# A fused attention, expert and gate kernel on one core: rounding, low halves and operand making re-divided between VectorE and GpSimd, and respread over the stages

## Chip, cores and metric

One Trainium2 chip, one core. The metric is the device time of one launch in microseconds. Engines are named as in the profile: PE is TensorE (PEld its weight loads), DVE VectorE, ACT ScalarE, POOL GpSimd, SP SyncE; SP issues most transfers.

## What is computed

All in fp32, B=4, H=8, S=576, D=64, so N=2304 tokens of 512:

```python
k_p, v_p = mean of 8 neighbours of k, v
x = softmax(q @ k_p.T / sqrt(D)) @ v_p                    # attention, heads side by side: (2304, 512)
p = domain_probs / domain_probs.sum(-1)
x = sum over 4 experts of p[:, e] * (relu(x @ w1[e]) @ w2[e])      # w1 512x1024, w2 1024x512
out = (((x @ g_w1) * (x @ g_w2)) @ w3) @ w_out            # g_w1, g_w2 512x1024, w3 1024x1024, w_out 1024x512
```

Four of the inputs (`moe2_*`) arrive as 8-byte floats.

## The kernel before

**Exact products.** A matrix is held as a high and a low half in the fast fp32 form; `hi_lo` (L111) makes the high half on ACT and the low half as source minus high on DVE, or on the engine that the caller names. `mm3` (L106) makes each product of three matmuls. One function serves all tiles, so the low halves all have line 113.

**Rounding.** The 8-byte inputs are made into 4-byte ones on the chip, in 80 steps of 256 columns. `Rounding.step` (L208) loads two words per number (`din`), runs seven DVE instructions (L219 to L225) on `dtmp`, two buffers, and one add on POOL (L226). The result is stored by the *next* step's `flush` (L202): `wo` and the gate columns directly (L752), w3 transposed on DVE first (L256). Where steps stand is written by hand: a table of hooks in the attention stage, `at_s1` and `at_s2` in the experts. The first 48 steps (`SCRATCH`) are `w_out` and w3, then come 32 for the gate weights.

**Attention and expert 0** run interleaved over six batches of 384 tokens, eight units of first and second products each, with a hook before and after each unit's second product. Hooks hold the pieces of attention: scores, exponentials, sums, the quotient on POOL (L433), transpositions, and `attend`, whose product PE writes and `hi_lo` splits into the batch's `x`. `START` sets the hook of each of the 18 tiles of 128 tokens. `accumulate0` (L723) evicts four banks at the end of a batch. At the end of the stage `weights_of` and `prepare_x` make the operands of expert 1.

**Experts 1 to 3** run over four batches of 576 tokens. First products use seven products instead of eight (`seven`, L664): `weights_of(j)` (L589) takes two tiles `raw` of w1, makes four sums on DVE into one tile `s` (L600 to L603; the tag "t" has one buffer, which `prepare_x` shares) and splits everything into a set of seven operands; `prepare_x` (L624) does the like for a batch of `x` (L630 to L633) and stores it for later experts, which read it back with `fetch_x` (L650). `seven` evicts on DVE (L670); ACT makes relu twice, POOL the low half `h` (L700). Second products run in two halves of eight steps, each on four of the eight PSUM banks, evicted by `accumulate` (L730 on DVE, an adding transfer from POOL at L731). The **last batch** of an expert also makes the next expert's four weight sets, in the first products from the second group on, and splits its eight rows of w2 in the second half. In the last batch of expert 3 the sets are the gate's, the rows are `wo`, and `prepare_x` makes the gate's first two operands.

**w3 stage and gate.** `w3_rows` (L937) splits sixteen rows of w3; 192 matmuls make w3 @ w_out. The gate stage makes two halves of the hidden columns, four batches each, first products with `seven` and then 128-token tiles of output, copied by ACT in the first half (L1046) and added by DVE in the second (L1043). Half 0's last batch (`swap`) makes the second half's weight sets.

Each engine runs its instructions in the order in which the program records them, and SP its transfers; a wait holds up all that stands behind it. A low half that the change moves is a call with or without `nc.gpsimd`:

```python
hi_lo(*(t[:, at:at + m].rearrange("p a b c -> p (a b c)") for t in wop_t[j]), src, nc.gpsimd)
```

## Time and profile before

| | before |
|---|---|
| median of 3 runs (lowest to highest) | 1362.57 us (1360.78 to 1363.24) |
| the profiled execution: its time, its span | 1363.6 us, 1361.9 us |
| PE busy | 1221.3 us, 90% |
| DVE, ACT, POOL busy | 843.9 us (62%), 372.4 (27%), 542.4 (40%) |
| mean granted TensorE clock | 0.949 |

The page gives busy times per engine and the groups of instructions; a busy PE is not PE at its peak. The table of windows gives, for a stretch of the span, each engine's busy time and the granted clock, 1.00 for 2.4 GHz and 0.5 for 1.2. The timeline names, behind each instruction, how long its engine stood idle before it and what ended that. Where a wait has several causes, the one that came last is named.

### The profile page before, as it was taken

What the parts mean: (1) busy time and instruction counts of PE and PEld (TensorE: products, weight loads), DVE (VectorE), ACT (ScalarE), POOL (GpSimd) and SP (SyncE); (2) the same over time, 40 slices, a digit from 0 to 9 for tenths busy, and PEclk for the clock granted to TensorE, in tenths of its full rate; (3) what the DMA queues carried; (4) which work ended last, traced back from release to release, by engine and by line L of the source; (5) the groups of instructions that cost most, each with busy time, mean ns of one, the idle gap of its engine ahead of it and who ended that gap; (6) DMA issues with size and microseconds to landing.
All of it is one profiled execution on the core that took longest, in us unless ns stands there. A gap on an engine that the chain in (4) does not pass through costs nothing.

```text
span 1361.9 us, 21447 instructions
## 1 busy us (share of the span) xinstructions
PE 1221.3 (90%) x7953; PEld 1156.3 (85%) x7953; DVE 843.9 (62%) x1765; ACT 372.4 (27%) x659; POOL 542.4 (40%) x534
## 2 busy tenths in 40 slices
PE   6889798989889987799998689999839999979997
PEld 4777787889889987799998689999828999879996
DVE  5758877745678774577675675767430776555453
ACT  3333122222423414323214131132322332321110
POOL 5544443142635536234336343344634332442121
PEclk8899898999899998899999889999869999989999
DMA  8776544443664763756663746655255144755441
GB/s 194 202 177 171 165 122 126 115 116 109 216 186 99 234 183 100 218 175 162 138 213 73 227 133 172 194 175 133 82 127 201 36 188 178 260 192 183 156 168 62
DMA packets 176508, 216.51 MB, mean 159 GB/s; under 512 B 50892, under 2 KB 126996, under 8 KB 176404
## 3 DMA queue, kind: packets, MB, share of 16 engines
q1 hardware_dynamic: 160564, 196.27, 44.8%
q0 software_dynamic: 15840, 18.88, 9.4%
...
HBM read 133.80 MB, written 81.30 MB: 158 GB/s over the span
## 4 chain that ended last, share of the span: by engine, by line
PE 60%; DVE 14%; DMA 10%; issue 7%; POOL 5%; SPq 3%; ACT 2%; DVEq 0%; POOLq 0%; ACTq 0%
PE g L107 9%; PE g L108 9%; PE g L109 9%; PE s L107 9%; PE s L109 9%; PE s L108 9%; POOL wl L113 2%; DMA stage<-in_q_dram 1%; DMA raw<-in_moe_w_dram 1%; DMA gate<-dtmp 1%; DMA din<-in_moe_w_dram 1%; PE w L108 1%; PE w L109 1%; PE x_ps L454 1%; PE w L107 1%
## 5 line engine op out<-in xcount | busy, mean ns | idle before, releaser
L107 PE MATMUL s<-xol,wh 128*128 128x288 f32 x980 | 297.6, 304 | 40.0 <-DVE part L730 34.6
L107 PE MATMUL g<-h,w2h 128*128 128x288 f32 (+1 forms) x960 | 298.5, 311 | 30.4 <-DVE u L670 17.5
L109 PE MATMUL s<-xoh,wh 128*128 128x288 f32 x980 | 295.1, 301 | 0.0
L108 PE MATMUL g<-h,w2l 128*128 128x288 f32 (+1 forms) x960 | 294.7, 307 | 0.0
L109 PE MATMUL g<-h,w2h 128*128 128x288 f32 (+1 forms) x960 | 294.5, 307 | 0.0
L108 PE MATMUL s<-xoh,wl 128*128 128x288 f32 x980 | 294.3, 300 | 0.0
L107 PEld LDWEIGHTS s<-xol,wh 128*128 128x128 f32 x980 | 188.6, 192 | 44.0 <-DVE part L730 36.3
L107 PEld LDWEIGHTS g<-h,w2h 128*128 128x128 f32 x960 | 184.2, 192 | 36.4 <-DVE u L670 18.5
L700 POOL TENSOR_TENSOR h<-c,h 128x576 fp32r<-128x576 f32 x96 | 140.1, 1480 | 143.7 <-ACT c L699 121.8
L108 PEld LDWEIGHTS s<-xoh,wl 128*128 128x128 f32 x980 | 189.2, 193 | 0.2
L109 PEld LDWEIGHTS s<-xoh,wh 128*128 128x128 f32 x980 | 188.8, 193 | 0.0
L108 PEld LDWEIGHTS g<-h,w2l 128*128 128x128 f32 x960 | 184.3, 192 | 0.0
L109 PEld LDWEIGHTS g<-h,w2h 128*128 128x128 f32 x960 | 184.0, 192 | 0.0
L226 POOL TENSOR_TENSOR dtmp<-dtmp 128x256 f32<-128x256 f32 x80 | 60.6, 757 | 240.1 <-DVE dtmp L225 199.0
L113 POOL TENSOR_TENSOR g<-c,g 128x576 fp32r<-128x576 f32 x32 | 47.3, 1479 | 196.4 <-ACT g L112 196.4
L698 ACT ACTIVATE h<-c 128x576 fp32r<-128x576 f32 x96 | 65.0, 677 | 197.7 <-DVE c L670 197.7
L672 ACT ACTIVATE x<-s 128x288 f32<-128x288 f32 x80 | 31.7, 397 | 197.6 <-PE s L109 197.5
L670 DVE TENSOR_TENSOR c<-s,v 128x288 f32<-128x288 f32 x160 | 69.1, 455 | 24.4 <-PE s L109 16.5
L670 DVE TENSOR_TENSOR u<-s,x 128x288 f32<-128x288 f32 x80 | 36.2, 453 | 75.7 <-ACT x L672 65.7
L107 PE MATMUL g<-xl,w 128*128 128x384 f32 x192 | 70.5, 367 | 0.5 <-DVE xl L113 0.5
L699 ACT ACTIVATE c<-c 128x576 f32<-128x576 f32 x96 | 65.8, 686 | 5.9
L108 PE MATMUL g<-xh,w 128*128 128x384 f32 x192 | 67.4, 351 | 0.0
...
## 6 DMA issues: line engine op xcount, KB each, us to landing
...
```

Of the source, the lines that this page charges most:

```text
L107: nc.tensor.matmul(ps, lh, rl, start=first, stop=False)
L108: nc.tensor.matmul(ps, ll, rh, start=False, stop=False)
L109: nc.tensor.matmul(ps, lh, rh, start=False, stop=last)
L113: (lo_eng or nc.vector).tensor_tensor(lo, src, hi.bitcast(F32), op=ALU.subtract)
L226: nc.gpsimd.tensor_tensor(a, a, b, op=ALU.add)
L454: nc.tensor.matmul(px[a * D:(a + 1) * D, off:off + n], vp_t[b][:NK, 2 * hp + a], at_t[i, hp // 2][:NK, 2 * (hp % 2) + a, off:off + n], sta ...
L670: nc.vector.tensor_tensor(to, one, two, op=ALU.add)
L672: nc.scalar.activation(x, product(j, A11, B11), AF.Copy)
L698: nc.scalar.activation(h[:, 0], r, AF.Relu)
L699: nc.scalar.activation(r, r, AF.Relu)
L700: nc.gpsimd.tensor_tensor(h[:, 1], r, h[:, 0].bitcast(F32), op=ALU.subtract)
```

## The change

- The add that ends a rounding step (L226) goes from POOL to DVE. The low halves in `prepare_x` (of `xr`), of A11, A12 and A22 in `weights_of`, of w3's rows, and of w2's rows in expert 1's first batch go from POOL to DVE. The low half of the four sums `s` and `h` stay on POOL.
- Rounding steps: in the attention stage 20 instead of 24, five in each of four batches; in expert 1's first three batches three each instead of five; in those of experts 2 and 3 seven instead of six; none in a last batch (expert 2's had five); three in the w3 stage and two in each of the first three batches of the gate stage, which had none.
- In a last batch set 0 is made in the first products, in two pieces, and sets 1 to 3 in the second products, a piece at every second step. The swap batch of the gate stage makes one piece per group and the rest afterwards; at the end of the attention stage the sets move by two units.
- Of the gate's first operands, one is made at step 3 of expert 3's last second products and one after them; two rows of w3 are split before the last eviction, a third of the rows in tiles with the tag "c".
- Attention: each batch makes the three tiles and the product of the next one, at the same places in all batches; pooling of k and v moves with it.

```diff
--- before.py
+++ after.py
@@ -225,3 +225,3 @@
             nc.vector.scalar_tensor_tensor(b, l, 2.0 ** -52, b, op0=ALU.mult, op1=ALU.mult)
-            nc.gpsimd.tensor_tensor(a, a, b, op=ALU.add)
+            nc.vector.tensor_tensor(a, a, b, op=ALU.add)
             self.done = a, sink
@@ -549,18 +549,19 @@
         hooks[6] = [(None, probs_T)]
-        START = {t: 3 * (t - TPB) if t < 2 * TPB else 6 + (55 * (t - 2 * TPB + 1)) // 12 for t in range(TPB, NTILE)}
-        for t, at in START.items():
-            hooks[at] += do_scores(t) + do_exps(t)
-            if t > TPB:
-                hooks[at + 1] += do_qT(t + 1)
-            one, two = do_normalise(t)
-            hooks[at + 1].append(one)
-            hooks[at + 2].append(two)
-            one, two = do_turn(t)
-            hooks[at + 4].append(one)
-            hooks[at + 5].append(two)
-            if t % TPB == TPB - 1:
-                for n, piece in enumerate(do_attend(t // TPB)):
-                    hooks[at + 5 + n].append(piece)
+        for i in range(1, NB):
+            base = PER * (i - 1)
+            for o in range(TPB):
+                t, at = TPB * i + o, base + 3 * o
+                hooks[at] += do_scores(t) + do_exps(t)
+                if t > TPB:
+                    hooks[at + 1] += do_qT(t + 1)
+                one, two = do_normalise(t)
+                hooks[at + 1].append(one)
+                hooks[at + 2].append(two)
+                one, two = do_turn(t)
+                hooks[at + 4].append(one)
+                hooks[at + 5].append(two)
+            for n, piece in enumerate(do_attend(i)):
+                hooks[base + 11 + n].append(piece)
         hooks[1] = do_qT(TPB + 1) + hooks[1]
-        for b, at_v, at_k in ((1, 3, None), (2, 25, 16), (3, 43, 33)):
+        for b, at_v, at_k in ((1, 3, None), (2, 30, 20), (3, 50, 39)):
             for n, piece in enumerate(do_v(b, GP)):
@@ -577,3 +578,3 @@
         for i in range(1, NB - 1):
-            for at in (0, 2, 5, 7, 10, 12, 14) if i < NB - 2 else (0, 3, 5):
+            for at in (0, 3, 6, 9, 14):
                 also.setdefault(PER * i + at, []).append(lambda: rounding.step(SCRATCH))
@@ -590,5 +591,5 @@
 
-            def split(src, at, m):
+            def split(src, at, m, eng):
                 src = src.rearrange("p a b c -> p (a b c)") if len(src.shape) == 4 else src.rearrange("p a c -> p (a c)")
-                hi_lo(*(t[:, at:at + m].rearrange("p a b c -> p (a b c)") for t in wop_t[j]), src, nc.gpsimd)
+                hi_lo(*(t[:, at:at + m].rearrange("p a b c -> p (a b c)") for t in wop_t[j]), src, eng)
 
@@ -603,7 +604,7 @@
                 nc.vector.tensor_tensor(s[:, 3], left[:, 2:], s[:, 1], op=sub)
-                split(left, A11, 2)
-                split(right[:, 2:], A22, 1)
+                split(left, A11, 2, nc.vector)
+                split(right[:, 2:], A22, 1, nc.vector)
                 stream.fill()
             if n != 0:
-                split(parts.pop(j), S1, 4)
+                split(parts.pop(j), S1, 4, nc.gpsimd)
 
@@ -633,4 +634,4 @@
             nc.vector.tensor_tensor(t[:, 3], r[:, 1, 0], t[:, 1], op=sub)
-            hi_lo(bh[:, 0], bl[:, 0], r[:, 0, 0], nc.gpsimd)
-            hi_lo(bh[:, 1:], bl[:, 1:], r[:, 1], nc.gpsimd)
+            hi_lo(bh[:, 0], bl[:, 0], r[:, 0, 0])
+            hi_lo(bh[:, 1:], bl[:, 1:], r[:, 1])
             hi_lo(th, tl, t)
@@ -821,9 +822,10 @@
                 at = n - (NB - 1) * FC
-                if at in (-3, -1, 1, 3):
-                    weights_of((at + 3) // 2, 0)
-                if at in (-2, 0, 2, 4):
-                    weights_of((at + 2) // 2, 1)
-                if at == 2:
+                for j, n0, n1 in ((0, -1, 0), (1, 1, 2), (2, 4, 5), (3, 5, 6)):
+                    if at == n1:
+                        weights_of(j, 1)
+                    if at == n0:
+                        weights_of(j, 0)
+                if at == 1:
                     load_x(x_d, 0, 0)
-                if at == 5:
+                if at == 3:
                     prepare_x(0, slot(), kept_d[0][0][0])
@@ -862,3 +864,17 @@
 
-        DONE = SCRATCH + 4 * FC
+        w3_hs = {}
+
+        def w3_rows(n):
+            (r, _), = stream.take()
+            if n % 3 == 1:
+                t = [partpool.tile([P, 512], F32R, tag="c", name="w3h", bufs=3) for _ in range(2)]
+            else:
+                t = (partpool.tile([P, 2, 512], F32R, tag="part", name="w3h") if n % 3 == 2
+                     else late["t"].tile([P, 2, 512], F32R, tag="xr", name="w3h", bufs=2))
+                t = [t[:, 0], t[:, 1]]
+            hi_lo(t[0], t[1], r[:, 0])
+            stream.fill()
+            w3_hs[n] = t
+
+        DONE = SCRATCH + 4 * FC - 9
         quota = rounding.steps
@@ -869,4 +885,4 @@
                 take_x()
-                at_s1 = (2,) if not last_b else ()
-                at_s2 = () if final else (1, 4, 7, 10, 13) if e > 1 else (5, 8, 11, 14) if not last_b else ()
+                at_s1 = () if last_b else (0, 2) if e > 1 else ()
+                at_s2 = () if last_b else (1, 4, 7, 10, 13) if e > 1 else (5, 10, 13)
                 quota += len(at_s1) + len(at_s2)
@@ -888,3 +904,3 @@
                     if e == 1 and b == 0:
-                        stream.split()
+                        stream.split(nc.vector)
                         stream.split(nc.vector)
@@ -895,6 +911,4 @@
                         rounding.step(quota)
-                    if last_b and j > 1:
-                        weights_of(j - 2, 1)
-                    if last_b and j:
-                        weights_of(j - 1, 0)
+                    if last_b and j in (1, 2):
+                        weights_of(0, j - 1)
                     if j == 0:
@@ -911,5 +925,2 @@
                         fetch_x(kc, slot(), store[kc])
-                if last_b:
-                    weights_of(NJ - 2, 1)
-                    weights_of(NJ - 1)
                 for half in range(2):
@@ -925,3 +936,7 @@
                         step = half * FC + n
-                        if make and step in (0, 2):
+                        if last_b and step in (0, 2, 4, 6, 8, 10):
+                            weights_of(step // 4 + 1, step % 4 // 2)
+                        if final and step == 3:
+                            prepare_x(0, slot(), store[0])
+                        if make and not final and step in (0, 2):
                             prepare_x(step // 2, slot(), store[step // 2])
@@ -931,2 +946,5 @@
                             stream.split(nc.vector)
+                    if final and half == 1:
+                        w3_rows(0)
+                        w3_rows(1)
                     accumulate(e, 2 * b + half, pss)
@@ -934,15 +952,4 @@
 
-        w3_hs = {}
-
-        def w3_rows(n):
-            (r, _), = stream.take()
-            shape = [P, 2, 512]
-            t = (partpool.tile(shape, F32R, tag="part", name="w3h") if n % 3 == 2
-                 else late["t"].tile(shape, F32R, tag="xr", name="w3h", bufs=2))
-            hi_lo(t[:, 0], t[:, 1], r[:, 0], nc.gpsimd)
-            w3_hs[n] = t
-
+        prepare_x(1, slot(), kept_d[1][0][1])
         take_x()
-        w3_rows(0)
-        w3_rows(1)
         n = 0
@@ -957,5 +964,7 @@
                     sl = slice(o * P, (o + 1) * P)
-                    mm3(ps, t[:, 0, sl], t[:, 1, sl], wh[:, 0], wl[:, 0], fc == 0, fc == FC - 1)
+                    mm3(ps, t[0][:, sl], t[1][:, sl], wh[:, 0], wl[:, 0], fc == 0, fc == FC - 1)
                 if n == FC:
                     put_away()
+                if n in (5, 8, 11):
+                    rounding.step(DONE + 3)
                 n += 1
@@ -991,2 +1000,4 @@
                 if swap:
+                    rounding.flush()
+                    assert rounding.finished()
                     stream_gates(1)
@@ -1008,6 +1019,4 @@
                         nc.gpsimd.tensor_copy(edge[:, j, :, P - S % P:], g_t[j][:, :, :P - S % P])
-                    if swap and j > 1:
-                        weights_of(j - 2, 1)
                     if swap and j:
-                        weights_of(j - 1, 0)
+                        weights_of(j // 3, int(j == 2))
                     if j == 1:
@@ -1018,4 +1027,5 @@
                 if swap:
-                    weights_of(NJ - 2, 1)
-                    weights_of(NJ - 1)
+                    weights_of(1, 1)
+                    weights_of(2)
+                    weights_of(3)
                 first = b * S - (S % P if b % 2 else 0)
@@ -1068,2 +1078,4 @@
                         put_away()
+                    if half == 0 and not swap and m in (0, 2):
+                        rounding.step(SCRATCH + 4 * FC)
                 if not last:
```

Two places of the order; the lines of the change are one or more further down than those of before (L601 for L600, L731 for L730). On DVE, in the second products of expert 2's last batch: before, from the last weight set on (`s` are its sums, `raw` the w1 tiles, `dtmp` and `din` of rounding), then the change, from the third set through the eviction of the first half (`part<-g`) to the start of the fourth.

```order
L600 TENSOR_TENSOR s<-raw 128x256
L601 TENSOR_TENSOR s<-s,raw 128x256
L602 TENSOR_TENSOR s<-raw 128x256
L603 TENSOR_TENSOR s<-raw,s 128x256
L219 TENSOR_SCALAR dtmp<-din 128x256
L220 TENSOR_SCALAR dtmp<-din 128x256
L221 TENSOR_SCALAR dtmp<-dtmp 128x256
L222 TENSOR_SCALAR dtmp<-dtmp 128x256
L223 SCALAR_TENSOR_TENSOR dtmp<-dtmp 128x256
L224 TENSOR_SCALAR dtmp<-dtmp 128x256
L225 SCALAR_TENSOR_TENSOR dtmp<-din,dtmp 128x256
L219 TENSOR_SCALAR dtmp<-din 128x256
```

```order
L601 TENSOR_TENSOR s<-raw 128x256
L602 TENSOR_TENSOR s<-s,raw 128x256
L603 TENSOR_TENSOR s<-raw 128x256
L604 TENSOR_TENSOR s<-raw,s 128x256
L113 TENSOR_TENSOR wl<-raw,wh 128x512
L113 TENSOR_TENSOR wl<-raw,wh 128x256
L731 TENSOR_TENSOR part<-g_7830,p 128x288
L731 TENSOR_TENSOR part<-g_7831,p 128x288
L731 TENSOR_TENSOR part<-g_7832,p 128x288
L731 TENSOR_TENSOR part<-g_7833,p 128x288
L601 TENSOR_TENSOR s<-raw 128x256
L602 TENSOR_TENSOR s<-s,raw 128x256
```

Before, three rounding steps stood between the sets and the first half's eviction; now a set does, with its two low halves, and no step.

On SP, in the same batch: the transfers around the fetch of the next batch's operands (`xoh`, `xol` from `kept`; `raw` of 4x128 columns is w1, of 512 is w2), before and then now.

```order
L713 DMA p<-p 128x288 x2
L132 DMA raw<-in_moe_w_dram 128x4x128 x4
L130 DMA raw<-in_moe_w_dram 128x512 x2
L650 DMA xoh<-kept 128x864
L650 DMA xoh<-kept 128x1152
L650 DMA xol<-kept 128x864
L650 DMA xol<-kept 128x1152
L650 DMA xoh<-kept 128x864
L650 DMA xoh<-kept 128x1152
L650 DMA xol<-kept 128x864
L650 DMA xol<-kept 128x1152
L130 DMA raw<-in_moe_w_dram 128x512 x2
```

```order
L714 DMA p<-p 128x288 x2
L132 DMA raw<-in_moe_w_dram 128x4x128 x2
L651 DMA xoh<-kept 128x864
L651 DMA xoh<-kept 128x1152
L651 DMA xol<-kept 128x864
L651 DMA xol<-kept 128x1152
L651 DMA xoh<-kept 128x864
L651 DMA xoh<-kept 128x1152
L651 DMA xol<-kept 128x864
L651 DMA xol<-kept 128x1152
L132 DMA raw<-in_moe_w_dram 128x4x128 x2
L130 DMA raw<-in_moe_w_dram 128x512 x8
```

Before, all w1 pieces and two w2 rows were issued ahead of the fetch; now two w1 pieces and all eight w2 rows stand behind it.

## Rows read from the trace of the kernel before

**Rows 1.** Windows: start:end, us, busy by engine (instructions), clock, DMA share, GB/s.

```profile
34.00:332.60 298.60, 270.21 (x1536) 246.39 (x1537) 205.40 (x436) 84.14 (x169) 119.12 (x158) 0.95 0.55 146
...
357.00:522.20 165.20, 150.07 (x1082) 148.66 (x1081) 122.11 (x264) 51.03 (x85) 76.13 (x62) 0.96 0.65 180
522.20:588.60 66.40, 53.08 (x362) 52.14 (x361) 35.18 (x65) 23.66 (x40) 31.54 (x23) 0.90 0.48 131
614.00:636.50 22.50, 22.50 (x170) 22.50 (x169) 16.43 (x40) 9.19 (x16) 10.63 (x8) 1.00 0.49 88
636.50:662.00 25.50, 25.50 (x195) 25.50 (x194) 16.60 (x45) 2.63 (x4) 7.44 (x8) 1.00 0.73 227
733.40:810.90 77.50, 54.91 (x363) 53.99 (x362) 47.16 (x100) 21.68 (x37) 34.70 (x26) 0.85 0.47 137
954.60:1057.20 102.60, 75.14 (x386) 65.15 (x385) 32.98 (x51) 30.50 (x50) 47.19 (x34) 0.85 0.44 136
...
1057.20:1163.80 106.60, 103.62 (x661) 96.34 (x661) 76.21 (x129) 32.41 (x56) 35.81 (x36) 1.00 0.35 129
...
1091.90:1152.90 61.00, 58.99 (x398) 55.99 (x397) 41.08 (x71) 17.12 (x31) 17.85 (x18) 1.00 0.52 202
1163.80:1235.40 71.60, 63.34 (x397) 59.06 (x397) 39.76 (x78) 18.14 (x34) 30.16 (x26) 0.93 0.60 213
```

The busy times in a row stand in the order PE, PEld, DVE, ACT, POOL.

**Rows 2.** Page, part 1: busy us (share of the span) of VectorE and GpSimd.

```profile
PE 1221.3 (90%) x7953; PEld 1156.3 (85%) x7953; DVE 843.9 (62%) x1765; ACT 372.4 (27%) x659; POOL 542.4 (40%) x534
```

**Rows 3.** Waits of PE over the span: total us, times, longest.

```profile
PE s L107 <- DVE part L730: 34.6, 7, 9.4
...
PE g L107 <- DVE u L670: 20.7, 5, 4.6
PE w L107 <- DVE wo L113: 19.3, 1, 19.3
PE g L107 <- DVE part L723: 9.8, 3, 6.2
PE at_ps L439 <- POOL e L433: 8.8, 6, 3.6
```

**Rows 4.** Timeline of DVE, end of expert 2: start, us, what, [idle before].

```profile
768.73 0.29 DVE L219 TENSOR_SCALAR dtmp<-din 128x256 uint32<-128x256 uint32 x1 [7.22 <-DMA gate<-dtmp]
...
789.20 1.54 DVE L730 TENSOR_TENSOR part<-g,p 128x288 f32<-128x288 f32 x4
```

**Rows 5.** Timeline of DVE, expert 3's last batch: two sets.

```profile
968.69 1.50 DVE L600 TENSOR_TENSOR s<-raw 128x256 f32<-128x256 f32 x1 [5.86 <-POOL wl L113]
...
975.34 1.48 DVE L600 TENSOR_TENSOR s<-raw 128x256 f32<-128x256 f32 x1 [3.61 <-POOL wl L113]
```

**Rows 6.** Timeline of DVE: single durations, POOL silent, silent, and busy.

```profile
560.44 0.69 DVE L113 TENSOR_TENSOR w2l<-raw,w2h 128x512 fp32r<-128x512 f32 x1 [7.77 <-ACT w2h L112]
...
756.82 0.41 DVE L603 TENSOR_TENSOR s<-raw,s 128x256 f32<-128x256 f32 x1
...
946.41 1.65 DVE L603 TENSOR_TENSOR s<-raw,s 128x256 f32<-128x256 f32 x1
```

**Rows 7.** A window of 2 us in the fetch of an undisturbed batch.

```profile
592.00:594.00 2.00, 2.00 (x17) 2.00 (x16) 1.93 (x5) 1.32 (x3) 1.87 (x2) 1.00 1.04 421
```

**Rows 8.** Timeline of PE, w3 stage: first matmuls of two rows.

```profile
1019.79 0.39 PE L107 MATMUL w<-wo,w3h 128*128 128x512 f32 x1
...
1022.57 0.39 PE L107 MATMUL w<-wo,w3h 128*128 128x512 f32 x1
```

**Rows 9.** Timeline of DVE, expert 1's second batch: both `prepare_x`, then rounding.

```profile
420.50 0.45 DVE L630 TENSOR_TENSOR t<-xr 128x288 f32<-128x288 f32 x1
...
433.76 0.44 DVE L256 STREAM_TRANSPOSE turned<-dtmp 128x256 f32<-128x256 f32 x1
...
441.63 0.45 DVE L256 STREAM_TRANSPOSE turned<-dtmp 128x256 f32<-128x256 f32 x1 [0.92 <-POOL dtmp L226]
```

## The prediction

> **What bounds the kernel now.** I read the page's engine shares first, then the matmul engine's waits, then a table of windows cut at the program's stages, and last the vector engine's timeline inside the worst of them. The matmul engine (PE) is the bound: in an undisturbed batch of an expert it never idles, 22.5 us for the first products and 25.5 for the second [rows 1]. The vector engine (DVE) is busy for 62% of the span and GpSimd (POOL) for 40% [rows 2], so neither is full; what costs time is their order. PE's longest waits [rows 3] all end at DVE or POOL: 34.6 us for the evictions of the second products (L730), 20.7 for those of the first (L670), 19.3 for the rows of `wo` before the w3 stage, 9.8 for L723 and 8.8 for the softmax quotient that POOL makes (L433). The stage table [rows 1] says where: expert 1's last batch with the next first products takes 66.4 us instead of 48, expert 2's 77.5 instead of 48, expert 3's last second products with the w3 stage 102.6. In these windows the granted clock is 0.90 and 0.85 where the undisturbed batch has 1.00; after a long stall PE runs for some us at 1.2 instead of 2.4 GHz, so a stall costs more than its length.
>
> The timeline gives two causes. At the end of expert 2 a rounding step's first instruction stood 7.22 us for the store of an earlier step, and the evictions behind it in DVE's queue (four, 1.54 us together, L730) came that much late [rows 4]. In every last batch DVE cannot begin the next set of weights (L600) until POOL has finished with the one tile `s`: 5.86 us of standing, and 6.65 us from one set to the next [rows 5].
>
> **The change part by part.** Prices first. A two-input DVE operation on 256 columns took 0.41 us alone and 1.65 us beside a POOL operation; the low half of a 512-column row took 0.69 [rows 6]. So the moved work costs DVE, uncontended: 80 rounding adds x 0.41 = 33 us, 20 weight sets x 1.1 = 22, 16 `prepare_x` x 1.2 (288 and 576 columns at the same rate) = 19, 16 rows of w3 x 0.69 = 11, 4 rows of w2 = 3; 88 us together, and POOL loses more than that. DVE's share becomes some 74%. All of it has to lie beside PE's work; where it does and where not is the sum.
>
> *Ends of experts 1 and 2.* The rounding steps leave expert 2's last batch, and three of the four weight sets move from the first products into the second. On DVE: the last first-product evictions end about 3 us into the second products, three sets at no more than today's 6.65 us [rows 5] end at 23 of 25.5 us, the eight w2 rows (5.5 us) fit between them except the last, which cannot start before PE's last matmul reads its old tile; then 0.69 + 1.54 us of eviction. PE meanwhile has four products (3.2 us) in the other four banks. On paper nothing stalls. SP now issues the fetch of the next `x` (eight transfers, 4.1 MB) directly at the end of the first products and the late w1 pieces and w2 rows behind it; at 421 GB/s [rows 7] the fetch needs 10 to 12 us of the 25.5, so the rows are in time, barely. I leave 2 us at each end: gains 66.4 - 48 - 2 = **16.4** and 77.5 - 48 - 2 = **27.5**. Bounds: 9 (a transfer wait like the 7.77 us for a w2 row that expert 1 already has [rows 6] stays) and the whole excess.
>
> *Expert 3's last batch and w3.* PE reaches w3 when the first w3 row is split. DVE has 3 + 3 x 6.65 us of sets and one `prepare_x` (4.4 us: four subtractions at 0.41, low halves of 288, 576 and 1152 columns) before the `wo` rows, and behind them eight `wo` rows that arrive by transfer as raw tiles come free; so the first w3 row is split some 29.4 us after the second products began, 3.9 after they end. The other `prepare_x` stands behind it. The stage itself is 16 rows of twelve matmuls; one row took 2.78 us (1019.79 to 1022.57 [rows 8]), all 44.5. I add 6 us for the low clock after the idle and for the third row, whose tile `part` waits for the last accumulation's transfer. 25.5 + 3.9 + 44.5 + 6 = 79.9 against 102.6: **22.7**, bounds 14 and 28. The three rounding steps put into w3 lie in an idle DVE.
>
> *Expert 1, from the second products of its first batch to the first products of its last.* 165.2 us [rows 1] for three of each, 144 undisturbed. Here `prepare_x` twice took 13.3 us (420.50 to 433.76) and each rounding step stood 0.92 us for POOL's add [rows 9]. With the low halves on DVE and POOL silent two take 8.8; steps fall from five to three a batch. DVE's chain in the second products goes from some 28 us to some 20, under 25.5. In the first batch DVE splits both w2 rows per group and stays slightly slow, so of 21.2 I take **18**, bounds 9 and 21.
>
> *Gate stage.* The swap batch, with the tiles after it and the next first products, takes 71.6 us where the same stretch two batches earlier takes 61.0 [rows 1]. The sets no longer stand between the first products, but the last two still delay the copies out of PSUM: I keep 4.5 of 10.6, a gain of 6. Against it, six rounding steps (2.9 us each) enter three batches where DVE has 76.2 of 106.6 us [rows 1]; most is covered by the 30 us left, I charge 1 us a batch. Net **3**, bounds -11 (all 17.4 us on the path) and 9.
>
> *Attention stage.* 298.6 us at clock 0.95. Five rounding steps a batch instead of seven, spread, the add on DVE: POOL's quotient (8.8 us of PE's waits) no longer queues behind an add that waits for DVE, and the longest wait for L723, 6.2 us, which follows a run of rounding steps, goes; the other 3.6 of its 9.8 [rows 3], waits for the transfer out of `part`, stay. Five batches now carry three tiles each, and the last attention product is finished half a unit before it is used, on a DVE that has 205.4 of 298.6 us. 6 + 6 + 3 of clock = **15**, bounds 0 and 22.
>
> Sum: 16.4 + 27.5 + 22.7 + 18 + 3 + 15 = 102.6. The profiled execution took 1363.6 us (span 1361.9); 1363.6 - 102.6 = 1261. The median of the runs is 1.0 lower: **1260**. A measurement of this kernel can tell about 0.2%, 2.7 us, from no change. The low bounds add up to a gain of 41 (1322), the high ones to 127 (1236); they will not all fall on one side.
>
> **The skill weighed.** Moving work from POOL to the busier DVE: the row says DVE takes 0.41 us alone and 1.65 beside POOL, so taking the POOL side away shortens DVE's neighbours too, and the sum uses 0.41. The Trainium skill (Perfetto Trace Analysis, "Optimizing Scalar/DVE Operations") advises the other direction, to hand work from a saturated DVE to ScalarE or even GpSimd, and adds that between DVE and GpSimd it may not help as they share a port; by it the change ends at the second rival's 1298. The trace agrees with its port remark (0.41 against 1.65).
>
> **Rivals.** (1) *Transfers take the place of the rounding.* For: expert 1's end has no rounding in its second products and PE still stood there; SP's queue puts ten transfers behind the fetch. Against: in the kernel before SP stands in front of that fetch until DVE has freed raw tiles, which the change lets it do earlier. Price: half of expert 1's 18.4 us, 9.2, at both ends instead of 2, and as much more as at one end, 7, at the `wo` rows: 1260 + 14 + 7 = 1281. (2) *DVE is full.* In the attention stage and in the gate stage its queue becomes PE's clock: no 15 there, 14.4 more for the rounding, half of expert 1's 18: 1260 + 15 + 14 + 9 = 1298. For: its shares of 0.69 and 0.71 in those windows before the work is added. (3) *Slower: the port.* If every moved operation meets a POOL operation at the contended 1.65 instead of 0.41, 88 us become some 350, and POOL's `h` (L700), which PE's second products need, waits in turn; it decides once more than 103 us of that come onto the path. At 40% on the path, 140 us: 1363.6 - 103 + 140, some 1400. Against: in the second products POOL is now nearly silent. The Trainium skill (SBUF — State Buffer, "Who interferes with whom") has the rule that two SBUF inputs on DVE and a reading GpSimd instruction lock each other out for a whole instruction. (4) *It only moves the waits*: each stall comes back under another name, 1363.
>
> **How the numbers follow.** Forecast 0.62 (own range 1243 to 1277), rival 1 0.16, rival 2 0.13, rival 3 0.05, rival 4 0.04. A range from 1240 to 1312 takes in the forecast, both milder rivals and most of the bounds. Faster: the first three, 0.91, and half of 4: 0.93; same 0.02; slower 0.05.
>
> **What would show it.** Right: the window from the end of expert 2's first products to the end of the next ones near 50 us, no L219 waiting for a gate store there, L600 waiting under 3 us for POOL, PE's wait for L730 under 10 us in all; w3 starting within 6 us of the last second product; POOL near 27%, DVE above 70%. Wrong: PE waiting for L730 while DVE waits for ACT and ACT for raw rows (rival 1); DVE over 90% of the attention or gate windows with PE waiting for L723, `h` or `g` (rival 2); POOL's 1.48 us for `h` and DVE's 0.45 us growing (rival 3).

## The result, and the profile after

The changed kernel takes 1286.02 us (median of 3 runs, 1283.71 to 1288.11) against 1362.57: a ratio of 0.944, 95% interval 0.9411 to 0.947, a gain of 76.6 us where 102.6 were forecast. The profiled execution is the median itself, 1286.02 us, with a span of 1284.2 us.

The page, part 1, answers to [rows 2]:

```profile
PE 1204.1 (94%) x7953; PEld 1140.8 (89%) x7953; DVE 886.9 (69%) x1937; ACT 373.2 (29%) x659; POOL 372.6 (29%) x362
```

POOL lost 169.8 us of busy time, DVE gained only 43.0. I had priced the moved work at 88 us of DVE. With the durations of both traces added up, the groups that gained instructions take 91 us more on DVE, and those that kept their number take 40 less, 32 of it in the sums of `weights_of` and `prepare_x` (`s` and `t`), which before stood beside a busy POOL at times, as the last line of [rows 6] shows. (Overlapping ends count twice in such sums, so the difference is 51 there and 43 on the page.)

Windows of the kernel after, cut at the same stages as [rows 1] (start:end, us, busy of PE, PEld, DVE, ACT, POOL, clock, DMA share, GB/s): attention; expert 1's middle; end of expert 1; the second products of a batch of expert 2; middle of expert 2; end of expert 2; middle of expert 3; its last second products with w3; the gate's first three batches; the swap batch.

```profile
35.10:319.00 283.90, 263.00 (x1536) 240.35 (x1537) 197.28 (x437) 84.06 (x169) 87.68 (x121) 0.96 0.57 148
342.50:490.60 148.10, 145.82 (x1083) 145.37 (x1082) 107.15 (x241) 51.27 (x85) 41.80 (x31) 0.99 0.64 180
490.60:540.50 49.90, 48.51 (x362) 47.97 (x362) 35.96 (x76) 23.64 (x40) 24.58 (x15) 1.00 0.62 180
592.90:620.60 27.70, 25.72 (x195) 25.49 (x194) 22.93 (x59) 2.63 (x4) 5.22 (x4) 1.00 0.78 228
540.50:694.80 154.30, 147.62 (x1081) 146.92 (x1081) 121.81 (x289) 36.95 (x63) 43.42 (x32) 0.98 0.64 169
694.80:744.20 49.40, 48.50 (x362) 47.97 (x361) 38.16 (x75) 23.17 (x39) 23.55 (x15) 1.00 0.62 184
744.20:893.70 149.50, 144.62 (x1082) 143.91 (x1081) 114.60 (x270) 36.75 (x62) 44.12 (x31) 1.00 0.63 182
893.70:983.80 90.10, 76.17 (x388) 65.04 (x387) 52.84 (x102) 31.49 (x52) 15.99 (x9) 0.91 0.50 155
983.64:1090.20 106.56, 104.14 (x662) 96.42 (x661) 87.73 (x178) 32.38 (x56) 22.82 (x24) 1.00 0.40 145
1090.20:1157.10 66.90, 62.47 (x398) 58.93 (x397) 41.46 (x97) 18.20 (x34) 21.80 (x18) 0.95 0.66 237
```

The ends of experts 1 and 2 are as clean as forecast (49.9 and 49.4 us, clock 1.00). But an ordinary batch of expert 2 is not undisturbed any more: its second products take 27.7 us where they took 25.5, and the middles of experts 2 and 3 are 9.5 and 5.8 us *longer* than before.

PE's waits, which answer to [rows 3] (total us, times, longest):

```profile
PE g L107 <- DVE u L671: 12.7, 7, 2.7
PE w L107 <- ACT w3h L112: 10.0, 2, 8.4
PE g L107 <- DVE part L724: 6.5, 1, 6.5
PE at_ps L439 <- POOL e L433: 4.0, 4, 2.0
PE w L108 <- DVE w3h L113: 3.9, 2, 3.7
...
PE s L107 <- DVE part L731: 1.4, 2, 0.9
```

The 34.6 us for the evictions of the second products have become 1.4. In their place stand seven waits for the evictions of the first (L671 is before's L670), six of them in the ordinary batches of experts 2 and 3. One such place on DVE, the first products of expert 2's second batch, with the two rounding steps after j = 0 and j = 2:

```profile
526.08 1.41 DVE L222 TENSOR_SCALAR dtmp<-dtmp 128x256 uint32<-128x256 uint32 x1
527.52 1.52 DVE L223 SCALAR_TENSOR_TENSOR dtmp<-dtmp 128x256 uint32<-128x256 uint32 x1
...
530.21 0.45 DVE L671 TENSOR_TENSOR u<-s,x 128x288 f32<-128x288 f32 x1
...
539.50 1.40 DVE L222 TENSOR_SCALAR dtmp<-dtmp 128x256 uint32<-128x256 uint32 x1
540.93 1.51 DVE L223 SCALAR_TENSOR_TENSOR dtmp<-dtmp 128x256 uint32<-128x256 uint32 x1
...
543.61 0.45 DVE L671 TENSOR_TENSOR u<-s,x 128x288 f32<-128x288 f32 x1
```

And POOL in the same stretch:

```profile
525.77 2.98 POOL L701 TENSOR_TENSOR h<-c,h 128x576 fp32r<-128x576 f32 x2 [2.09 <-ACT c L700]
...
539.18 2.99 POOL L701 TENSOR_TENSOR h<-c,h 128x576 fp32r<-128x576 f32 x2 [2.45 <-ACT c L700]
```

Each step starts just as POOL makes two `h`, some 1.5 us each, and two of its instructions take 1.4 to 1.5 us instead of 0.29 and 0.43, their times where POOL is silent (L222 at 973.07, in the w3 stage below). A step so lasts 4.9 us, from 525.39 to 530.29, and the last group's evictions begin at 543.61, 26.3 us after the first products did (517.30), when PE has been in the second ones for 3 us. The Trainium skill (SBUF — State Buffer, "Who interferes with whom") says that DVE and GpSimd exclude each other for a whole instruction where they need the shared port; the pairing of the long instructions with POOL's two agrees with that.

The stage times of all traces, as distances between the first matmuls of the stages (us; "e2 mid" is expert 2 from its first second products to the end of its last first products, "e2 end" from there to the next expert's second products; the gate goes to the end of the span):

| kernel | lead | attention | e1 mid | e1 end | e2 mid | e2 end | e3 mid | e3 last + w3 | gate |
|---|---|---|---|---|---|---|---|---|---|
| before | 34.1 | 298.5 | 165.3 | 66.4 | 144.8 | 77.4 | 143.7 | 102.7 | 304.7 |
| after | 35.1 | 283.9 | 148.1 | 49.9 | 154.3 | 49.4 | 149.5 | 89.9 | 300.6 |
| one step in first products | 32.3 | 284.5 | 148.1 | 50.5 | 154.4 | 50.3 | 157.0 | 91.3 | 301.4 |
| no step in w3 | 34.8 | 284.3 | 148.1 | 50.2 | 154.3 | 49.4 | 149.4 | 86.5 | 332.5 |
| both of these | 34.9 | 283.2 | 148.1 | 50.8 | 156.9 | 49.9 | 157.7 | 84.3 | 333.0 |
| add on POOL | 33.1 | 279.7 | 148.0 | 50.5 | 151.3 | 50.7 | 146.7 | 89.0 | 299.7 |
| sets in first products | 34.0 | 284.2 | 148.1 | 64.6 | 153.5 | 64.9 | 148.7 | 98.9 | 299.7 |
| old attention | 32.9 | 290.3 | 148.1 | 50.3 | 154.3 | 49.5 | 149.3 | 90.9 | 302.7 |
| before, free last batch | 34.6 | 295.6 | 167.0 | 65.2 | 152.5 | 62.5 | 156.6 | 103.0 | 305.4 |
| low halves on POOL | 33.1 | 285.3 | 152.3 | 55.2 | 151.6 | 53.2 | 148.2 | 94.8 | 311.0 |
| early stores | 33.7 | 284.2 | 150.3 | 51.1 | 181.6 | 49.2 | 152.1 | 92.1 | 300.5 |
| early stores, one step | 33.7 | 282.8 | 150.8 | 50.3 | 181.5 | 49.4 | 162.1 | 90.9 | 300.9 |
| add on POOL, rows in turns | 36.2 | 280.8 | 146.5 | 50.9 | 149.6 | 50.0 | 146.7 | 85.7 | 299.2 |
| and the steps spread | 34.1 | 279.9 | 157.9 | 50.3 | 145.2 | 50.5 | 146.0 | 85.7 | 299.4 |

The columns leave out expert 1's first first products: 23.4 to 24.3 us in all kernels but the one with the low halves on POOL, where they take 27.6. The lead, up to the first product of expert 0, varies by 4 us between kernels that are the same there, and the attention stage by 3 (298.5 and 295.6); differences of that size in whole times are read from the stages.

### The profile page after: what moved, and what is told of

The parts are those of the page before. It is cut to its first block, busy times and chain, and to the rows that moved or that the text cites. A ratio compares the mean times of both kernels' runs of the same rounds, so it can differ in the third digit from the quotient of the medians.

```text
span 1284.2 us, 21307 instructions
## 1 busy us (share of the span) xinstructions
PE 1204.1 (94%) x7953; PEld 1140.8 (89%) x7953; DVE 886.9 (69%) x1937; ACT 373.2 (29%) x659; POOL 372.6 (29%) x362
## 4 chain that ended last, share of the span: by engine, by line
PE 59%; DVE 16%; DMA 9%; issue 6%; POOL 5%; ACT 2%; SPq 2%; DVEq 0%; ACTq 0%; POOLq 0%
PE g L107 11%; PE g L109 11%; PE g L108 11%; PE s L107 7%; PE s L109 7%; PE s L108 7%; POOL h L701 2%; DVE c L671 2%; POOL wl L113 2%; DMA raw<-in_moe_w_dram 2%; DMA stage<-in_q_dram 1%; PE x_ps L454 1%; DVE dtmp L223 1%; DMA acc<-part 1%; DVE u L671 1%
## 5 line engine op out<-in xcount | busy, mean ns | idle before, releaser
L107 PE MATMUL g<-h,w2h 128*128 128x288 f32 (+1 forms) x960 | 298.5, 311 | 21.3 <-DVE u L671 12.7
L107 PE MATMUL s<-xol,wh 128*128 128x288 f32 x980 | 293.7, 300 | 7.5 <-DVE u L671 2.2
L109 PE MATMUL s<-xoh,wh 128*128 128x288 f32 x980 | 292.0, 298 | 0.0
L108 PE MATMUL s<-xoh,wl 128*128 128x288 f32 x980 | 291.0, 297 | 0.0
L107 PEld LDWEIGHTS s<-xol,wh 128*128 128x128 f32 x980 | 185.4, 189 | 10.4 <-DVE u L671 3.2
L108 PEld LDWEIGHTS s<-xoh,wl 128*128 128x128 f32 x980 | 185.8, 190 | 0.2
L109 PEld LDWEIGHTS s<-xoh,wh 128*128 128x128 f32 x980 | 185.6, 189 | 0.0
L671 DVE TENSOR_TENSOR u<-s,x 128x288 f32<-128x288 f32 x80 | 36.3, 454 | 79.0 <-ACT x L673 71.2
L732 POOL DMA_DIRECT2D acc<-part x24 | 29.1, 1213 | 208.9 <-DVE part L731 186.7
L671 DVE TENSOR_TENSOR c<-s,v 128x288 f32<-128x288 f32 x160 | 68.0, 455 | 19.2 <-PE s L109 11.1
L113 POOL TENSOR_TENSOR wl<-s,wh 128x1024 fp32r<-128x1024 f32 x20 | 49.1, 2457 | 76.1 <-ACT wh L112 76.1
L112 ACT ACTIVATE g<-c 128x576 fp32r<-128x576 f32 x32 | 22.0, 686 | 157.8 <-DVE c L988 157.8
```

The source lines that it names most:

```text
L107: nc.tensor.matmul(ps, lh, rl, start=first, stop=False)
L108: nc.tensor.matmul(ps, ll, rh, start=False, stop=False)
L109: nc.tensor.matmul(ps, lh, rh, start=False, stop=last)
L112: nc.scalar.activation(hi, src, AF.Copy)
L113: (lo_eng or nc.vector).tensor_tensor(lo, src, hi.bitcast(F32), op=ALU.subtract)
L671: nc.vector.tensor_tensor(to, one, two, op=ALU.add)
```

## Experiments

**The second step in the first products.**

```diff
-                at_s1 = () if last_b else (0, 2) if e > 1 else ()
-                at_s2 = () if last_b else (1, 4, 7, 10, 13) if e > 1 else (5, 10, 13)
+                at_s1 = () if last_b else (2,) if e > 1 else ()
+                at_s2 = () if last_b else (1, 3, 6, 8, 11, 13) if e > 1 else (5, 10, 13)
```

> One edit to the changed kernel: in experts 2 and 3 a batch's first products run one rounding step (after j = 2) instead of two (after j = 0 and 2); the seventh goes to the second products, six instead of five. Theory: the second step in the first products is what costs experts 2 and 3 15.3 us against my sum (stage times 154.3 and 149.5 us where 144.8 and 143.7 were before): it runs beside POOL's h, its two long instructions take 1.4 to 1.5 us instead of 0.3 to 0.4, and the evictions of the last first products come behind it. Then the waits of PE of 1.4 to 2.7 us at the start of the second products go, the two middles fall back to about 145 and 144, and the run takes 1271 to 1275. Rival 1, the add that now stands on DVE, or DVE's fill as such, is what costs: six steps in the second products then crowd DVE as much, the middles stay at 150 to 155 and the run at 1283 to 1289, or above if steps in the second products delay the sums. Rival 2, contention of any one step with POOL's h is enough: the waits stay at 2 us each and less than 4 us is gained.

Measured: 1299.61 us (1294.93 to 1300.64; ratio to before 0.9518, 0.9497 to 0.9539), slower than the changed kernel. The waits at the start of the second products did go (those products take 25.4 or 25.5 us in all six batches, together 16.4 us less than in the kernel after), so the second step is what made them. But PE now waits at the start of the next *first* products. That wait of PE, and DVE there, from expert 3 (start, us, what, [idle before]):

```profile
PE s L107 <- DVE part L731: 19.7, 8, 5.1
```

```profile
757.88 0.29 DVE L219 TENSOR_SCALAR dtmp<-din 128x256 uint32<-128x256 uint32 x1 [6.47 <-DMA gate<-dtmp]
...
774.11 0.29 DVE L219 TENSOR_SCALAR dtmp<-din 128x256 uint32<-128x256 uint32 x1 [3.82 <-DMA gate<-dtmp]
...
776.95 1.54 DVE L731 TENSOR_TENSOR part<-g,p 128x288 f32<-128x288 f32 x4
```

A step writes one of two buffers `dtmp`; it may start when the store of two steps back has landed, and that store is issued only at the step between. Steps closer together than a landing wait for it, and the sums (L731) stand behind. My theory missed that price. Rival 1 had room for it in its last clause, steps that delay the sums, without the cause; its other half, that not the second step costs, falls with the waits that went. Seven steps a batch have a bad place in both placements tried.

**The steps in w3.**

```diff
-                if n in (5, 8, 11):
-                    rounding.step(DONE + 3)
-                    if half == 0 and not swap and m in (0, 2):
+                    if half == 0 and not swap and m in (0, 1, 2):
```

> One edit to the changed kernel: the three rounding steps of the w3 stage go to the gate stage (one more in each of three batches). Theory: the third of them is what stops w3 for 3.69 us at 972 us: its first instruction waits on DVE for a store of gates that stands on SP behind the kept stores, and the halves of a w3 row stand behind it on DVE; with the low clock after it the step costs 5 to 7 us. Then the w3 stage takes 49 to 51 us where it took 55.7, the gate stage pays 0 to 2, and the run takes 1279 to 1283. Rival: the same kept stores hold the last raw row of w3, which landed at 972.8 too, so that PE waits there without any rounding step: the stage stays at 53 us or more and the run within 2.5 us of 1286.

Measured: 1316.70 us (1312.08 to 1319.73), 31 us slower than the changed kernel. The w3 half of the theory held: the stage takes 51.1 us (929.27 to 980.40) instead of 55.6, and the rival, a raw row that is late anyway, falls. In the kernel after, what stood there was this, on DVE, and on SP ahead of it:

```profile
972.34 0.29 DVE L219 TENSOR_SCALAR dtmp<-din 128x256 uint32<-128x256 uint32 x1 [8.20 <-DMA gate<-dtmp]
...
973.07 0.29 DVE L222 TENSOR_SCALAR dtmp<-dtmp 128x256 uint32<-128x256 uint32 x1
...
974.99 1.29 DVE L113 TENSOR_TENSOR w3h<-raw,w3h 128x512 fp32r<-128x512 f32 x2
```

```profile
957.69 0.90 SPq L641 DMA_DIRECT2D kept<-xoh  x2
958.64 2.12 SPq L641 DMA_DIRECT2D kept<-xol  x2
960.80 2.44 SPq L641 DMA_DIRECT2D kept<-xoh  x2
963.28 2.46 SPq L641 DMA_DIRECT2D kept<-xol  x2
965.78 1.20 SPq L199 DMA_DIRECT2D din<-in_moe_w_dram  x1
967.03 1.26 SPq L753 DMA_DIRECT2D gate<-dtmp  x1
```

Eight kept stores hold SP for 8 us, and the step's read and the earlier step's store stand behind them. The gate half was wrong: three steps in a batch cost 32 us, not 0 to 2. The reason is the same wait, once in each of the three batches (9.86, 9.54 and 9.29 us), with the evictions (L671) behind it:

```profile
1077.28 0.29 DVE L219 TENSOR_SCALAR dtmp<-din 128x256 uint32<-128x256 uint32 x1 [9.54 <-DMA gate<-dtmp]
...
1079.93 0.45 DVE L671 TENSOR_TENSOR u<-s,x 128x288 f32<-128x288 f32 x1
```

Both edits together:

> Both edits together: one rounding step in the first products of experts 2 and 3, none in w3. If both theories hold the gains add, 12 to 15 and 4 to 6 us, and the run takes 1264 to 1270, with the middles of experts 2 and 3 near 145 and 144 us and w3 at 49 to 51. By the rivals (DVE's fill costs, the raw row is late) it stays above 1280; if just one theory holds it takes 1271 to 1283.

Measured: 1324.41 us (1321.62 to 1327.79), far above the 1264 to 1270 of both theories. The stages are those of the two single runs within 3 us (table): w3 has its gain, and the losses in the middles and the gate stage add.

**The add.**

```diff
-            nc.vector.tensor_tensor(a, a, b, op=ALU.add)
+            nc.gpsimd.tensor_tensor(a, a, b, op=ALU.add)
```

> One edit to the changed kernel: the add that ends a rounding step goes back from DVE to POOL, as before the change. The prediction put this part of the change at a small gain, because the add is 1 us on POOL against 0.3 to 0.4 on DVE and a later step's first instruction waits for it. Theory: in the second products it costs nothing on either engine; in the first products POOL's add comes between the h of the last two groups, which the second products need: the waits at the start of the second products grow from 2 to 3 us or more, and the run takes 1286 to 1296. Rival: DVE is the engine short of time there, taking 0.4 to 1.0 us off each step relieves it, the waits shrink to 1 us or less and the run takes 1276 to 1283.

Measured: 1274.30 us (1272.99 to 1276.17; ratio 0.934, 0.9325 to 0.9355): 11.7 us *faster* than the changed kernel, in the rival's direction and 1.7 us beyond its range. PE's waits in this run:

```profile
PE w L107 <- ACT w3h L112: 10.8, 2, 9.1
PE g L107 <- DVE u L671: 8.4, 7, 2.0
...
PE at_ps L439 <- POOL e L433: 4.6, 5, 1.6
```

The waits for L671 shrink from 12.7 to 8.4 us, the longest from 2.7 to 2.0, less than the rival said. Of the gain, attention has 4.2 us, the two middles 5.8, w3 some 1; 2 us are the lead, which the add does not touch, so the add is worth some 10. In attention the three kernels with the add on POOL take 279.7 to 280.8 us and the changed ones with it on DVE 282.8 to 285.3 (old attention apart); which wait carries that was not found. The add is 0.42 us on DVE and 0.72 on POOL, yet it is cheaper there in the two middles: DVE is the engine on whose queue PE waits, and POOL has nothing to do at that point. The quotient (L433), which I had seen behind POOL's adds, waits no longer than with the add on DVE (4.6 us against 4.0).

**Sets, low halves and rounding apart.** Four parts of the change undone or done alone. The sets back in the first products of a last batch:

```diff
-                    if last_b and j in (1, 2):
-                        weights_of(0, j - 1)
+                    if last_b and j > 1:
+                        weights_of(j - 2, 1)
+                    if last_b and j:
+                        weights_of(j - 1, 0)
...
+                if last_b:
+                    weights_of(NJ - 2, 1)
+                    weights_of(NJ - 1)
...
-                        if last_b and step in (0, 2, 4, 6, 8, 10):
-                            weights_of(step // 4 + 1, step % 4 // 2)
```

> One part of the change undone: a last batch makes the next expert's weight sets in its first products again, as before (the low halves stay on DVE, the last batches still round nothing). Theory: the ends of experts 1 and 2 gained because the sets no longer crowd the first products and the stretch behind them. Then the end of expert 1 (second products of its last batch and first products of the next expert, 49.9 us after the change, 66.4 before) goes back to 60 to 66, that of expert 2 (49.4 after, 77.5 before) to 57 to 66, since the 28 us there are partly the rounding steps', the last batch of expert 3 with them, and the run takes 1305 to 1325. Rival: the low halves on DVE, which take POOL's queue away from the sets, carry the gain; then both ends stay within 4 us of 50 and the run takes 1284 to 1294.

Measured: 1324.04 us (1321.78 to 1326.77), inside the theory's range. The ends of experts 1 and 2 in this run, to be read against the third and the seventh window above:

```profile
490.26:554.76 64.50, 52.87 (x362) 52.29 (x362) 35.90 (x77) 23.00 (x39) 24.20 (x15) 0.87 0.50 141
708.20:773.30 65.10, 52.62 (x364) 51.51 (x363) 36.04 (x76) 22.32 (x38) 24.13 (x15) 0.90 0.49 140
```

DVE's work is the same (35.96 and 35.90 us at the first of them) and so is POOL's; only its place differs, and the stretch is 14.6 us longer at a lower clock.

The rounding alone, in the kernel before:

```diff
-                at_s2 = () if final else (1, 4, 7, 10, 13) if e > 1 else (5, 8, 11, 14) if not last_b else ()
+                at_s2 = () if last_b else (5, 8, 11, 14) if e == 1 else (1, 4, 7, 10, 13) if (e, b) == (2, 0) else (1, 3, 6, 8, 11, 13)
```

> The kernel before, with one part of the change alone: expert 2's last batch rounds nothing; its steps go to the other batches of experts 2 and 3, six in their second products instead of five. Theory: the steps' first instruction, which waits for a store behind others on SP, is a good part of what expert 2's end lost; then this end falls from 77.5 to 60 to 67 us, and the sets' place makes up the rest of the 28.1 us. Rival: the sets' place alone is what counts; the end stays above 73. In the middles six steps at two or three places' distance cost 4 to 12 us, as the run with six steps in the changed kernel has just shown (7.5 us in expert 3), so that the whole run takes 1352 to 1366 by the theory and 1364 to 1376 by the rival.

Measured: 1371.72 us (1368.68 to 1376.33; ratio 1.0083, 1.0055 to 1.0112). The end of expert 2 falls to 62.5 us, as the theory had it:

```profile
740.00:802.50 62.50, 52.67 (x363) 52.20 (x363) 35.86 (x66) 21.27 (x35) 29.71 (x21) 0.89 0.50 139
```

So of the 28.0 us there 14.9 are the rounding's and the rest the sets' and the low halves'; the run before gave 15.5 for the sets, which leaves 12.5. The two splits agree within 2.4 us. The whole time lies in the rival's range all the same: the middles lose 7.7 and 12.9 us to six steps in the second products, together more than the 4 to 12 that I had allowed, and with the add on POOL.

The low halves of weights and x back on POOL:

```diff
-                split(left, A11, 2, nc.vector)
-                split(right[:, 2:], A22, 1, nc.vector)
+                split(left, A11, 2, nc.gpsimd)
+                split(right[:, 2:], A22, 1, nc.gpsimd)
...
-            hi_lo(bh[:, 0], bl[:, 0], r[:, 0, 0])
-            hi_lo(bh[:, 1:], bl[:, 1:], r[:, 1])
+            hi_lo(bh[:, 0], bl[:, 0], r[:, 0, 0], nc.gpsimd)
+            hi_lo(bh[:, 1:], bl[:, 1:], r[:, 1], nc.gpsimd)
```

> One part of the change undone: the low halves of the weights' blocks and of the prepared x go back to POOL. Theory: in expert 1, where a batch's x is prepared beside its second products, POOL was the engine that came late; its three batches (148.1 us after, 165.3 before) go back to 154 to 162, the expert ends lose 2 to 6 us each, and the run takes 1296 to 1310. Rival, as for the rounding step's add, which is cheaper on POOL by 12 us: DVE is the engine that is short of time and POOL is free; then the stages keep their times or gain, and the run takes 1270 to 1284.

Measured: 1315.73 us (1310.98 to 1322.14), above the theory's range and far from the rival. Expert 1's middle loses just 4.2 us, where the theory had 6 to 14; more is lost elsewhere: 4.1 in expert 1's first first products, 5.3 and 3.8 us at the ends of experts 1 and 2, 4.9 in expert 3's last second products with w3, 10.4 in the gate stage. So the low halves have a part in the ends too, and the shares overlap: at the end of expert 1 the sets' 14.6 (64.5 against 49.9) and these 5.3 are more than the 16.5 gained. PE's longest wait in this run, then one of DVE's, first in the kernel after and then in this run:

```profile
PE w L107 <- ACT w3h L112: 15.2, 2, 13.1
```

```profile
DVE s L601 <- POOL wl L113: 17.1, 8, 2.9
```

```profile
DVE s L601 <- POOL wl L113: 27.1, 9, 4.5
```

Work of one kind, low halves, belongs on DVE here, and the add on POOL. What the traces show of the reason is who waits: the next set stands for POOL's split, 27.1 us here where it was 17.1 in the kernel after, while the add is first needed by the next step (with the add on POOL, DVE's transposition of L256 stood 10.1 us for it in the whole span). Those 10 us of standing are at most a third of the loss; the rest was not told apart, nor were the low halves of the weights and of x.

Attention as before, with the new rounding table (the hooks `START`, and the starts of values and keys, back to the old lines):

> One part of the change undone: the units of attention, with the values and keys that they need, stand where they stood before the change; the five rounding steps of a batch stay as changed. Theory: the attention stage gained 14.6 us by the even spacing of its units; then the first 319 us grow to 329 to 333 and the run takes 1296 to 1300. Rival: it gained by the rounding table (five steps in a batch at 3 to 5 units' distance, where seven stood), since DVE paces this stage; then it grows by less than 5 us and the run takes 1286 to 1291.

Measured: 1295.21 us (1292.95 to 1297.30). The stage takes 290.3 us instead of 283.9, so the spacing is worth 6.4 of the 14.6; that lies between theory and rival. By subtraction the other 8.2 are left for the table of steps, with the loss of 4.2 by the add inside them; no run changes that table alone, and the stage varies by 3 us.

**Earlier stores.** A `rounding.flush()` one group after a step in the first products, two places after one in the second, and ahead of the kept stores in w3 and the gate:

```diff
                     if j in at_s1:
                         rounding.step(quota)
+                    else:
+                        rounding.flush()
...
                         if step in at_s2:
                             rounding.step(quota)
+                        elif step - 2 in at_s2:
+                            rounding.flush()
...
+                if n in (7, 10, 13):
+                    rounding.flush()
                 if n == FC:
                     put_away()
```

> The changed kernel with one edit: a rounding step's store is issued two places after the step (in the first products one, in w3 two rows), not at the next step, so it stands in front of the kept stores and lands earlier. Steps, engines and order of the work stay. Theory: what stops w3 for 3.69 us, and DVE for 8.2 us there, is only the place of that store on SP; then w3 takes 49 to 51 us instead of 55.6. The middles of experts 2 and 3, where PE waits behind two steps in the first products and not for stores, stay at 152 to 155 and 148 to 150. Run: 1278 to 1282. Rival: SP, which has to stand until DVE has finished a step, holds back the raw rows and the fetch of x; the middles or w3 grow and the run takes 1287 or more.

Measured: 1323.30 us (1320.42 to 1325.67): the rival's number (1287 or more), though not by the transfers that it named: what SP holds back above all is the next step's read. The wait changed its name. In the kernel after, DVE's first instruction of a step stood 24.0 us for stores and 7.9 for reads of `din`; now it stands for reads, and PE behind it for the sums, where it had stood 1.4 us. The kernel after, then two lines of this run:

```profile
DVE dtmp L219 <- DMA gate<-dtmp: 24.0, 7, 8.2
```

```profile
DVE dtmp L219 <- DMA din<-in_moe_w_dram: 79.8, 18, 10.4
...
PE s L107 <- DVE part L731: 29.3, 8, 9.0
```

SP in expert 2, start, us, what, count, and the step on DVE that needs this read:

```profile
555.97 3.81 SPq L259 DMA_DIRECT2D w<-turned  x4
560.89 0.35 SPq L199 DMA_DIRECT2D din<-in_moe_w_dram  x1
```

```profile
564.16 0.29 DVE L219 TENSOR_SCALAR dtmp<-din 128x256 uint32<-128x256 uint32 x1 [9.59 <-DMA din<-in_moe_w_dram]
```

The read for the next step is issued in the step before, so it now stands behind a store that itself waits for DVE. In w3, which stays at 56.5 us, the same: the step there waits 7.43 us for its `din`, which like the store came behind the kept stores. The same edit on the kernel with one step in the first products:

> The run with one step in the first products and six in the second (1299.6 us), with stores issued two places after their step. Theory: there PE's waits at the start of the second products went, and the loss (1.5 to 5.1 us a batch at the start of the next first products) came from steps that stood 4 to 8 us for the landing of a store two steps back; with the store earlier these waits shrink below 1 us each, the middles of experts 2 and 3 fall to 145 to 148 us each, w3 to 49 to 51, and the run takes 1264 to 1274. Rival: seven steps are simply more than DVE can hold beside these batches wherever they stand; the middles stay above 152 and the run above 1283.

Measured: 1328.34 us (1327.88 to 1332.35), the middles 181.5 and 162.1 us. The theory falls with it. The rival's numbers hold, but its reason, that seven steps are too many wherever they stand, is not shown: whether a third buffer for `dtmp` would take the waits away stays open; it wasn't tried.

**Towards a better kernel.** In the kernel after, DVE's rows before w3, of which the last two are w3's first:

```profile
916.74 3.48 DVE L113 TENSOR_TENSOR wo<-raw,wo 128x512 fp32r<-128x512 f32 x2
921.63 2.69 DVE L113 TENSOR_TENSOR wo<-raw,wo 128x512 fp32r<-128x512 f32 x4 [1.40 <-ACT wo L112]
...
928.02 1.29 DVE L113 TENSOR_TENSOR w3h<-raw,w3h 128x512 fp32r<-128x512 f32 x2
```

The rows of `wo` and w3 in turns, on the kernel with the add on POOL:

```diff
-                    for _ in range(FC):
-                        split_wo()
                     for r0 in range(0, F, 512):
                         for fc in range(FC):
+                            if r0 == 0:
+                                split_wo()
...
-                        if last_b and half == 1:
+                        if last_b and half == 1 and not final:
...
-                        w3_rows(0)
-                        w3_rows(1)
+                        for n in range(2):
+                            stream.split(nc.vector)
+                            w3_rows(n)
...
+                if n + 2 < FC:
+                    stream.split(nc.vector)
                 if n + 2 < 2 * FC:
                     w3_rows(n + 2)
```

> The run with the rounding add on POOL (1274.3 us), with one more edit: the rows of wo and of w3 arrive and are split in turns (row n of w3 needs only row n of wo), so that w3 can start behind two rows of wo instead of eight. Theory: the 9.12 us that PE stands before w3 are the time until all eight rows of wo have arrived and been split; they shrink to 0 to 4 us, a wait of 2 to 5 us for the third row, whose tile is freed by the last sums' transfer, takes their place in part, and the low clock behind the idle shortens; the end of expert 3 and w3 together fall from 89.0 to 78 to 83 us and the run takes 1263 to 1269. Rival: DVE's queue in the last second products (three sets of weights, a prepared x, the sums) is what ends late, whatever the rows' order; less than 3 us is gained, 1271 to 1276.

Measured: 1270.83 us (1269.29 to 1272.31; ratio 0.9327, 0.9307 to 0.9347). PE enters w3 at once, but the third row comes late, as expected, and later than I said: one wait of 6.3 us stands where two made 10.8, and the stretch falls from 89.0 to 85.7 us, between theory and rival. The lead of this kernel is 3.1 us longer. And the twelve steps of the first products spread over three experts:

```diff
-                at_s1 = () if last_b else (0, 2) if e > 1 else ()
+                at_s1 = () if final else (0,) if last_b else (0, 2) if (e, b) == (E - 1, 0) else (2,)
```

> The run with the add on POOL and the rows of wo and w3 in turns (1270.8 us), with one more edit: the twelve rounding steps of the first products in experts 2 and 3, two in each of six batches, are spread: one in each batch of experts 1, 2 and 3 (after j = 2; after j = 0 in the last batches of experts 1 and 2), two only in expert 3's first; the second products keep their five and three. Theory: it is the second step in one batch's first products that delays the evictions, and a single one is free, as before the change; then the middles of experts 2 and 3 fall from 149.6 and 146.7 to 144 to 146 each, PE no longer waits over 0.5 us at the start of their second products, expert 1's middle stays within 2 us of 146.5, and the run takes 1261 to 1268. Rival: what is taken from experts 2 and 3 is paid in expert 1, where DVE also prepares x, and at the ends of experts 1 and 2, where it makes weights; the run takes 1269 to 1274.

Measured: 1272.41 us (1270.55 to 1275.90). Theory and rival each hold in part: the middle of expert 2 falls to 145.2 us and that of expert 3 to 146.0, but expert 1's grows by 11.4, with PE waiting 3.6 us in its first batch and 4.1 in its last. The two batches between them keep 22.5 and 25.4 us although DVE prepares x in their second products, so x is not what costs. In the first batch the step stands behind the split of two w2 rows, without a wait of its own. In the last one it stood for its read, which SP issued at 472.37, behind eight kept stores (461.01 to 472.28):

```profile
480.79 0.29 DVE L219 TENSOR_SCALAR dtmp<-din 128x256 uint32<-128x256 uint32 x1 [7.71 <-DMA din<-in_moe_w_dram]
```

So a single first-products step was free here where its read was in time and DVE had no split of rows beside it. The best measured kernels are this pair, 1270.8 and 1272.4 us, whose runs overlap; both beat the changed kernel by over 13 us.

## Why the prediction was right, and where it was off

The sign held, the mechanism at the ends of experts 1 and 2 held, and so did the wide range, 1240 to 1312. The forecast's own range, 1243 to 1277, was missed by 9 us: the gain came out 26 us smaller than the sum, and the first rival's 1281 and the second's 1298 lie nearer to 1286.0 than 1260. Two places make up the miss, the middles of experts 2 and 3 (15.3 us) and the stretch from expert 3's last second products through w3 (9.9). Three more terms came out right in size but not for the reasons given, which is luck. By its terms:

- *Ends of experts 1 and 2*: 16.5 and 28.0 us for 16.4 and 27.5. The two causes named were causes: no L219 waits for a store at the end of expert 2, L601 waits at most 2.9 us for POOL, and each part, undone or done alone, shows its share (14.6 to 15.5 us for the sets, 12.5 to 14.9 for the rounding). The low halves on DVE, which the term does not name, are worth 5.3 and 3.8 us there; the shares overlap.
- *Expert 1's middle*: 17.2 for 18. But the low halves carry only 4.2 of it, so my reason, `prepare_x` at 13.3 us, was the smaller part; the rest was not tested by itself. The add is not it (148.0 with it on POOL). The five steps a batch that became three are what is left to name; in the last run a fourth one, put into the first products, loses 11.4 us there, which points the same way.
- *Gate stage*: 4.1 for 3. The swap batch gained 4.7 us (71.6 to 66.9), where I took 6, and the three batches with steps took 106.6 us as before, where I had charged 3: two errors that nearly cancel. That the steps cost nothing is a balance too: with the low halves on POOL the three batches take 112.1 us, so this move paid for them. A third step a batch costs 32 us.
- *Attention*: 14.6 for 15, and yet not by its parts. The long wait for L723 did not go (6.5 us for 6.2), and POOL's quotient did not need the add gone. Spacing gave 6.4 us and the add took 4.2 back, so that by subtraction some 12 are left for the fewer steps, for which no run stands.
- *Expert 3's end and w3*: 12.8 for 22.7, below my lower bound of 14. Two sentences failed. The first is "3.9 after they end": w3 starts 8.4 us after the second products. My 29.4 us hold 27.4 for the sets and `prepare_x` and 2 for the `wo` rows, although eight rows at 0.69 are 5.5 by my own price. DVE was through with the sets and `prepare_x` sooner, 23.0 us after the second products began (893.70), but the `wo` rows then took 11.3: 7.5 of work, the first two rows drawn out beside POOL's last split (2.58 us from 917.10), and 3.7 of standing behind ACT, which stood for rows that had not arrived (the lines stand ahead of the run with the rows in turns). With the rows in turns the start is immediate. The second is "the three rounding steps put into w3 lie in an idle DVE": DVE was idle, but the third step waits 8.2 us at its head, and the w3 row behind it is what PE needs. The stage took 55.6 us, and 51.1 without steps, near the 44.5 + 6 of the sum.
- *What the sum left out*: the middles of experts 2 and 3, 15.3 us of loss. The change puts two rounding steps into their first products, and I let the steps pass under "all of it has to lie beside PE's work", although [rows 6] had the price of a DVE operation beside a busy POOL. The second step is the whole of it: with one step the second products are back at 25.4 or 25.5 us in all six batches with the add still on DVE, 16.4 us less. The add on DVE makes that step 5.8 us dearer. A single step is nearly free in these two experts (145.2 and 146.0 us in the last run); the sixth step in their second products is not.

The low halves of weights and x moved to DVE gave 30 us, with small losses in the middles of experts 2 and 3 (2.7 and 1.3); the add was part of the same sentence in my prices ("the moved work costs DVE, uncontended") and cost some 10 us. Of my signs of being right, w3's start within 6 us (8.4) and DVE above 70% (69%) failed, and POOL stands at 29% for 27; the others came. Of the rivals, the second (DVE full) names the direction of this miss, but not its place: DVE is nowhere near full, 69% of the span, and its order in two short stretches costs the time. The first (transfers) was right about the `wo` rows alone. The rule of the Trainium skill (Perfetto Trace Analysis, "Optimizing Scalar/DVE Operations"), that handing work from DVE to GpSimd might not help, decides neither case: the add gains 11.7 us on POOL, the low halves lose 29.7 there.
